# Quarter products for the last five pairs of the first layer, and a new order of work where attention ends

## The chip, the cores and the metric

One core of one Trainium2 chip runs the whole program. The metric is device time in microseconds (us) of one execution. Engines are named as in the profile: PE (TensorE matmul), PEld (its weight loads), DVE (VectorE), ACT (ScalarE), POOL (GpSimd), SP (SyncE, which issues the transfers).

## The reference

Attention (4 batches, 8 heads, 576 tokens, head size 64) whose scores are cut by a threshold near the row's maximum; then two feed-forward layers on 2304 tokens of width 512, all in fp32:

```python
scores = np.where(scores >= thresh, scores, -1e9)        # thresh = row max - tau
attn = exp(scores - max); attn = attn / (sum + 1e-09); x = attn @ v
x = (sigmoid(x @ w_gate) * (x @ w_val)) @ w_out          # d_ff 1536
h = x @ w_in                                             # d_ff 2048
y = where(h >= 1, h, where(h <= -1, 0, (h + 1)**2 / 4)) @ w2_out
```

The weights come in 64-bit floats as pairs of 32-bit words and are converted to fp32 on the chip.

## The kernel before

**Arithmetic.** Each fp32 operand of the layers is split in two parts of the matmul's input type (a high part, copied by ACT, and a low part, subtracted by DVE), and each product is three matmuls: high by high, high by low, low by high. Tokens go in three passes of 768 (T), each in two halves of 384 (HT).

**Attention** (`attention`, L200) is a generator over steps t. Pair p of heads takes five steps; N = 80 steps hold scores, and nine more drain the pipeline. `normalise` (L367) multiplies a pair's result by the reciprocal sums on POOL, 14 steps after the pair began, 12 for the last two pairs. `spread` (L361) loads the reciprocal sums, broadcast, from scratch memory: for the last pair at t = N + 3. `background` (L371) converts the first six blocks of weights in the gaps. At t = N the extraction of blocks 6 and 7 is issued and their conversion begun (`third`, four DVE operations at each of the following steps, L475).

**Layer 1** is `hidden` (L552), once for each of 36 steps s: three passes by twelve column tiles f of 128. For each half n it makes gate and value (`up`, L506: 12 matmuls of 384 columns each), the sigmoid of the gate on ACT (L567; L563 for the first tile, whose products `first_up`, L821, begins before attention has ended), the product of both on DVE (L571), its split (L572, L574). Between them it issues the split of the next tile's weights (`split_list`, L172: ACT L190, DVE L192) and some operations of `work`. Behind `hidden`, `down` (L781) multiplies the tile before by its block of w_out: 24 matmuls, four column tiles by 768 tokens, three times. Gate and value have one PSUM bank each: the next half may write one only when L567 or L571 has read it.

**Conversions** (`conversions`, L515) are the `work` of the steps: for each tile an extraction on ACT (L145), DVE operations L155 to L169, a store to scratch (`saved`). Eight operations go with each step of the first pass and six with the others (L879), so the generator ends before step 33. For layer 2 `w_sums` (L539) also makes four sums of quarter blocks of each pair of tiles and stores them in `tsaved`.

**Layer 2** is `pair` (L708), once for each of 24 pairs q: the product of 768 tokens by 512, with 512 by 256 weights, cut in 2 by 2 blocks, is made of seven block products (Winograd's form) in place of eight: 42 matmuls of 384 columns (`product`, L630), joined by copies on ACT (L730, L739) and sums on DVE (L715). `x_sums` and `w_sums` are the sums of blocks it needs. `value_steps` (L641) is the activation, `down_pair` (L764) 36 matmuls of 512 columns.

**Order of the side work in layer 2.** `due` (L665) queues steps for DVE and ACT with a time wanted, a first and a last slot and a cost; `fill` (L669) issues at four slots of a pair those that are eligible, in the order of their times, while they fit in the slot's room, and those whose last slot it is in any case. With `begin`, only steps with ACT work are taken, and the DVE step behind each gets time -1, ahead of all others. A slot is a place in the program, and each engine goes through its work in that order. At q = 0 the last tile's `down` and `finish` (L794, which copies layer 1's result out of PSUM) follow the first pair's products.

Of the kernel before, what the change touches and what calls it, by code (L numbers as in the profile page):

```python
# [10 lines left out]
F32 = mybir.dt.float32  # L11
# [18 lines left out]
def kernel(  # L30
# [63 lines left out]
    raws, wsp, pools, wsp_n, highs = {}, {}, {}, [], {}  # L94
# [105 lines left out]
    def attention():  # L200
# [166 lines left out]
        def normalise(p, s):  # L367
            x, c = x_of(p), slice(s * HS, s * HS + HS)
            nc.gpsimd.tensor_tensor(x[:, c], x[:, c], rbs[:, p % 2 * S :][:, c], op=ALU.mult)
# [33 lines left out]
        for p in range(NP):  # L403
            for i, (r, a, b) in (rounds if p + 1 < NP else final).items():
                parts.setdefault(p * U + i, []).append((p, r, range(a, b)))
        for t in range(N + 9):
# [56 lines left out]
            if t == N + 3:  # L463
                spread(NP - 1)
# [9 lines left out]
            if t > N:  # L474
                run(itertools.islice(third, 4))  # L475
            if t == N + 2:
                assert next(third, None) is None
                st2.close()
                ps_o.close()
            yield t - N, False  # L480

    def ffn(att):


        with ExitStack() as st:
# [7 lines left out]
            HC = HK * P  # L493

            def split_xs(ph, t, a, b, ks=range(KD)):

                x = xflat[:, : 2 * KD * T].rearrange("p (k i t) -> i p k t", k=KD, i=2)
                xh, xl = xsp[ph, t] = x[0], x[1]
                for c in ks:
                    src = xall[:, c, t * T + a : t * T + b]  # L500
                    nc.scalar.activation(xh[:, c, a:b], src, AF.Copy)
                    yield
                    nc.vector.tensor_tensor(xl[:, c, a:b], src, f32(xh[:, c, a:b]), op=ALU.subtract)
                    yield

            def up(ph, t, f, n, i, ps, ks=range(KD)):  # L506
                ih, il = wsp[ph, t, f][:2]
                xh, xl = xsp[ph, t]
                c = slice(n * HT, n * HT + HT)
                for kk in ks:  # L510
                    nc.tensor.matmul(ps, ih[:, i, kk], xh[:, kk, c], start=(kk == 0), stop=False)  # L511
                    nc.tensor.matmul(ps, ih[:, i, kk], xl[:, kk, c], start=False, stop=False)  # L512
                    nc.tensor.matmul(ps, il[:, i, kk], xh[:, kk, c], start=False, stop=(kk == KD - 1))  # L513

            def conversions():  # L515


                for j, (ph, f, gs) in enumerate(todo):
# [6 lines left out]
                    for m, _ in enumerate(ops):  # L525
                        if m == 3 + len(gs):
                            for g in todo[j + 2][2] if j + 2 < len(todo) else ():
                                load_w(todo[j + 2][0], g)
# [10 lines left out]
            def w_sums(j):  # L539

                b11, b21, b12, b22 = (w[:, i * HC : (i + 1) * HC] for w in w2s for i in range(2))
                t23, t14 = (x[:, 2 * KD * P :] for x in highs.values())
                t2, t3, t1, t4 = (x[:, i * HC : (i + 1) * HC] for x in (t23, t14) for i in range(2))
                for n, (o, a, b) in enumerate(((t1, b12, b11), (t2, b22, t1), (t3, b22, b12), (t4, b21, t2))):
                    nc.vector.tensor_tensor(o, a, b, op=ALU.subtract)
                    if n == 1:
                        yield
                for i, x in enumerate((t23, t14)):
                    nc.sync.dma_start(out=tsaved[j][:, i * 2 * HC : (i + 1) * 2 * HC], in_=x)
                yield  # L550

            def hidden(t, f, nxt, work):  # L552
# [5 lines left out]
                for n in range(2):  # L558
                    c = slice(n * HT, n * HT + HT)
                    act = hp_.tile([P, HT], F32, tag="act", name="act")  # L560
                    if (s := (0, t, f, n)) in early:
# [9 lines left out]
                    nc.vector.tensor_tensor(act, pv, act, op=ALU.mult)  # L571
# [14 lines left out]

            BX = 2 * HK * HT
            PRODUCTS = ((0, 0, 0, 1), (1, 1, 1, 1), (0, 2, 3, 0), (1, 3, 4, 1), (0, 4, 5, 1), (1, 5, 6, 0), (0, 6, 2, 0))

            def x_block(i):  # L590
                t = xmore[:, i * BX : (i + 1) * BX] if i < 3 else xflat[:, (i - 3) * BX :][:, :BX]
                return (t[:, : BX // 2], t[:, BX // 2 :])

            def x_sums(t):

                a11, a12, a21, a22 = (
# [4 lines left out]
                xops[t] = (a11, a12, s2, a21, s1, a22, s4)  # L601
# [4 lines left out]
            def x_split(t, i):  # L606
                a = xops[t][i]
# [3 lines left out]
            def w_split(q, i):  # L611
                w0, w1 = w32[q]
                src, a = ((w0[:, : 2 * HC], 0), (w1[:, HC : 2 * HC], 2 * HC), (tsum, 3 * HC))[i]
# [3 lines left out]
            def wout(q, i):  # L617
                s = (2 * q + i) % 4
                return wouts[s][:, 0], wouts[s][:, 1]
# [42 lines left out]
            LEN = lambda q: 11 if q == 0 else 15  # L662
            start = lambda q: sum(LEN(i) for i in range(q))

# [29 lines left out]
            def due_x(t, early=0):  # L694
                q = t * NQ
                for i in range(early, 7):
                    first = 4 * (q - 1) + (1, 1, 2, 3, 3, 3, 3)[i]
                    last = 4 * q - 1 if i < 2 else 4 * q + 1
                    due(first, last, split_steps(start(q) + i - 1, 0.84, 0.7, *x_split(t, i)))

            def due_w(q):
                at = start(q)
                for i, (when, first, last, cost) in enumerate(
                    ((-1, 4 * q - 3, 4 * q - 1, 0.6), (1.3, 4 * q - 1, 4 * q + 1, 0.32), (1, 4 * q - 1, 4 * q - 1, 1.1))
                ):
                    due(first, last, split_steps(at + when, cost, cost - 0.1, *w_split(q, i)))

            def pair(q):  # L708

                t, j = divmod(q, NQ)  # L710
                ps = [ps_a.tile([P, 512], F32, tag=f"a{i}", name="pu")[:, :HT] for i in range(2)]
                c = [(sqs[:, 1], vals[:, 0])[q % 2], (vals[:, 1], rbs, early_raw[1])[q % 3][:, :T]]
# [4 lines left out]
                more, last = q + 1 < NPASS * NQ, j == NQ - 1  # L717
                if more:
                    due_w(q + 1)
                if j == NQ - 4 and t + 1 < NPASS:  # L720
                    for i, w in enumerate(x_sums(t + 1)):
                        due(4 * q, 4 * (q + 3) - 1, [(start(q + 1) + 8 + 8 * i, 0.84, 0, True, w)])
                if last and more:
                    due_x(t + 1)
                at = start(q + 1) + 7
                for i in range(2):
                    src = w32[q][i][:, KD * P : 2 * KD * P]
                    due(4 * q, 4 * q + 5, split_steps(at - 1.8 + 0.3 * i, 0.6, 0.5, *wout(q, i), src))
# [4 lines left out]
                fill(4 * q + 1, 1.5, 1.3, small=True)  # L733
                if more:
                    load_sums(q + 1)
                if q + 2 < NPASS * NQ:
# [3 lines left out]
                fill(4 * q + 2, 0, 2.2, small=True, begin=True)  # L740
                product(3, ps)
                add(u3, ps[1], u2)
                product(4, ps)
                add(c[1][:, t1], ps[0], u3)
                product(5, ps)
                add(c[0][:, t1], ps[1], u2)
# [233 lines left out]
```

## Time and profile before

| | us |
|---|---|
| runs shown: median (lowest to highest of 3) | 1105.19 (1103.47 to 1106.47) |
| the profiled execution | 1104.5 |
| its span, first to last instruction | 1102.7 |
| attention, to the first matmul of layer 1 | about 256 |
| layer 1, to the first product of layer 2 | about 455 |
| layer 2 | about 391 |

The views are the page (shares of the whole span), the busy time by stretch, the chain of work that ended last, the timelines of single engines, and groups of instructions by line and shape. In a timeline a bracket is the idle time just before an instruction and what ended it. Times count from the span's start.

### The profile page before, as it was taken

To read this page: it belongs to the slowest core of one execution; us is meant where nothing else is said; L and a number is where in the kernel's file an instruction comes from. 1 tells how busy PE (TensorE), PEld (TensorE's weight loads), DVE (VectorE), ACT (ScalarE), POOL (GpSimd) and SP (SyncE) were. 2 spreads that over 40 slices of the span, in tenths; PEclk is the share of its full clock that TensorE was granted. 3 is DMA by queue.
4 is the path that set the end of the run, shared out by engine and by line. 5 is a ranking of instruction groups with operands and counts; after the bars stand their busy time and mean duration, and the time that the engine had idled before them with its cause. 6 is when DMAs were issued, how large, how long until landed. Compare 5 with 4: busy or idle time off the path is not lost.

```text
span 1102.7 us, 18536 instructions
## 1 busy us (share of the span) xinstructions
PE 1082.9 (98%) x6996; PEld 933.3 (85%) x6996; DVE 844.2 (77%) x1489; ACT 614.8 (56%) x1000; POOL 152.7 (14%) x315
## 2 busy tenths in 40 slices
PE   8999999999999999999999999999999999999998
PEld 6666666667899999999999999988898898888887
DVE  7999999997999988767686744576767767776663
ACT  6888888886343444333353322565566655665653
POOL 4556666552000000000000000000000000000000
PEclk9999999999999999999999999999999999999999
DMA  5344344413855566545654342223232423233301
GB/s 157 70 100 79 93 99 100 102 34 103 277 199 179 176 214 218 175 150 175 202 172 151 116 153 77 77 77 125 86 114 75 165 105 115 96 134 115 115 20 58
DMA packets 65146, 139.17 MB, mean 126 GB/s; under 512 B 9616, under 2 KB 35872, under 8 KB 65056
## 3 DMA queue, kind: packets, MB, share of 16 engines
q1 hardware_dynamic: 64912, 137.98, 39.2%
q8 instruction: 55, 0.90, 0.3%
q14 instruction: 35, 0.29, 0.1%
q10 hardware_dynamic: 144, 0.00, 0.0%
HBM read 111.15 MB, written 26.81 MB: 125 GB/s over the span
## 4 chain that ended last, share of the span: by engine, by line
PE 85%; ACT 7%; DVE 5%; issue 3%; POOL 0%; DVEq 0%; POOLq 0%; ACTq 0%
PE y L771 14%; PE pu L636 14%; PE y L789 13%; PE pgv L511 9%; PE pgv L512 9%; PE pgv L513 9%; PE av L338 6%; PE w L253 5%; PE w L306 4%; ACT ex L274 2%; PE w L249 1%; ACT sqs L645 1%; ACT sqs L646 1%; ACT hh L654 1%; DVE s L262 1%
## 5 line engine op out<-in xcount | busy, mean ns | idle before, releaser
L511 PE MATMUL pgv<-xflat,win 128*128 128x384 f32 x560 | 187.9, 336 | 3.0 <-DVE act L571 1.8
L512 PE MATMUL pgv<-xflat,win 128*128 128x384 f32 x560 | 187.9, 335 | 0.0
L513 PE MATMUL pgv<-xflat,win 128*128 128x384 f32 x560 | 187.8, 335 | 0.0
L771 PE MATMUL y<-wout,hh 128*128 128x512 f32 x576 | 184.1, 394 | 0.0
L789 PE MATMUL y<-hh,wout 128*128 128x512 f32 (+1 forms) x576 | 146.5, 336 | 0.0
L771 PEld LDWEIGHTS y<-wout,hh 128*128 128x128 f32 x576 | 108.2, 188 | 24.5
L262 DVE TENSOR_SCALAR_CACHE_REDUCE s<-w,nscale 128x576 f32<-128x576 f32 x144 | 112.2, 812 | 9.7 <-PE w L253 7.6
L571 DVE TENSOR_TENSOR act<-pgv,act 128x384 f32<-128x384 f32 x70 | 38.8, 554 | 105.2 <-PE pgv L513 104.9
L572 ACT ACTIVATE hh<-act 128x384 fp32r<-128x384 f32 x72 | 38.0, 528 | 141.7 <-DVE act L571 141.7
L771 PE MATMUL y<-wout,hl 128*128 128x512 f32 x288 | 113.6, 395 | 0.0
L282 DVE SCALAR_TENSOR_TENSOR p<-s,mx,ex 128x576 f32<-128x576 f32 x144 | 111.6, 807 | 0.0
L511 PEld LDWEIGHTS pgv<-xflat,win 128*128 128x128 f32 x560 | 105.6, 188 | 5.0 <-DVE act L571 2.1
L274 ACT ACTIVATE ex<-s,mx 128x576 f32<-128x576 f32 x144 | 104.3, 766 | 6.3 <-DVE s L262 5.9
L789 PEld LDWEIGHTS y<-hh,wout 128*128 128x128 f32 x576 | 98.1, 188 | 11.3
L512 PEld LDWEIGHTS pgv<-xflat,win 128*128 128x128 f32 x560 | 105.5, 188 | 1.6
L636 PE MATMUL pu<-xflat,win 128*128 128x384 f32 x576 | 105.2, 337 | 1.4 <-DVE sqs L715 1.1
L567 ACT ACTIVATE act<-pgv 128x384 f32<-128x384 f32 x70 | 34.2, 489 | 128.7 <-PE pgv L513 128.6
L513 PEld LDWEIGHTS pgv<-xflat,win 128*128 128x128 f32 x560 | 105.7, 189 | 0.0
L636 PEld LDWEIGHTS pu<-xflat,win 128*128 128x128 f32 x576 | 100.6, 188 | 3.1 <-DVE sqs L715 2.0
L789 PE MATMUL y<-hl,wout 128*128 128x512 f32 (+1 forms) x288 | 97.1, 337 | 0.0
L265 POOL TENSOR_SCALAR mx<-mx,tau_b 128x1 f32<-128x1 f32 x144 | 87.4, 607 | 54.7 <-DVE s L262 54.5
L253 PE MATMUL w<-qk 64*128 64x288 f32 x512 | 88.2, 430 | 2.9 <-DVE s L262 2.9
(153 smaller groups left out, 1866.0 us busy)
## 6 DMA issues: line engine op xcount, KB each, us to landing
words<-in_moe_w_out_dram SPq DMA_DIRECT2D x26, 512.0 KB
wmore<-saved SPq DMA_DIRECT2D x24, 512.0 KB
tsum<-tsaved SPq DMA_DIRECT2D x24, 512.0 KB
w<-saved SPq DMA_DIRECT2D x24, 512.0 KB
w<-saved SPq DMA_DIRECT2D x14, 768.0 KB
words<-in_moe_w_in_dram SPq DMA_DIRECT2D x16, 512.0 KB
saved<-w SPq DMA_DIRECT2D x16, 512.0 KB
wmore<-saved SPq DMA_DIRECT2D x10, 768.0 KB
```

The costliest lines, as they stand in the source:

```text
L253: nc.tensor.matmul(w[:, s, :HS], t[es, 0, u * P : u * P + P], t[es, 1, c], start=True, stop=True)
L262: nc.vector.tensor_scalar(t[:, e], w[:, :, :HS], nscale, None, op0=ALU.mult, op1=ALU.min, accum_out=mx[:, 0, e : e + 1])
L265: nc.gpsimd.tensor_scalar(mx[:, 1, e : e + 1], mx[:, 0, e : e + 1], tau_b, None, op0=ALU.add)
L274: nc.scalar.activation(ex[:, e], t[:, e], AF.Exp, scale=-1.0, bias=mx[:, 0, e : e + 1])
L282: nc.vector.scalar_tensor_tensor(pr[:, e], t[:, e].rearrange("p a b -> p (a b)"), mx[:, 1, e : e + 1], ex[:, e].rearrange("p a b -> p (a b ...
L338: nc.tensor.matmul(av[e * D : e * D + D, :n], vs[p % 3][:, e, c], rt[r][:, e, c] if c < nf else rl[r], start=c == 0, stop=c == nf,)
L511: nc.tensor.matmul(ps, ih[:, i, kk], xh[:, kk, c], start=(kk == 0), stop=False)
L512: nc.tensor.matmul(ps, ih[:, i, kk], xl[:, kk, c], start=False, stop=False)
L513: nc.tensor.matmul(ps, il[:, i, kk], xh[:, kk, c], start=False, stop=(kk == KD - 1))
L636: nc.tensor.matmul(ps[bank], l[:, k], r[:, k], start=bool(new) and k == m == 0, stop=k == HK - 1 and m == 2, skip_group_check=True,)
L771: nc.tensor.matmul(y[b], l[:, ts_], r, start=first and m == 0, stop=last and m == 2)
L789: nc.tensor.matmul(at(y, a, b), l[:, ds_], r[:, c], start=new and m == 0, stop=last and m == 2, skip_group_check=True,)
```

## The change

The last five pairs of column tiles of layer 1 (third pass, f = 2 to 11) no longer go through `hidden`. `stage` takes the place of `pair`: ten stages g come ahead of the 24 pairs of layer 2, an even one for the gates of a pair of tiles and an odd one for its values, each with seven block products of 42 matmuls. One `down` of layer 1 follows each stage from the second on, and two follow stage 10, the first pair of layer 2. The sums of weight blocks are made from the fp32 weights beside the stage before (`w_sums(g + 1)`), for layer 1 and for the first pass of layer 2, which stores them for the later passes. Gates go through the sigmoid, values through `gated_steps`. Four of the seven blocks of x are already in the tile `xflat` by its new layout or are made in its place.

Conversions now end before step 24: six operations at the first step, nine at the second, eight at each later one. Where attention ends, the whole of `third` is issued at t = N + 1, the split of tile 1's weights at step 1 in one go, then the sigmoid and product of the first half of tile 0. The last two pairs are normalised on DVE, one half with each of the steps 12 to 15; the last `spread` and the two stores of tiles 0 and 1 go behind step 1, and the loads of blocks 12 and 13 come early.

The diff, cut to its core:

```diff
-                for j in (12, 14):
-                    pn, un = divmod(t - j - i, U)
-                    if un == 0 and 0 <= pn < NP and (pn < NP - 2) == (j == 14):
-                        normalise(pn, i)
+                pn, un = divmod(t - 14 - i, U)
+                if un == 0 and 0 <= pn < NP - 2:
+                    normalise(pn, i)
...
-            if t == N + 3:
-                spread(NP - 1)
...
-            if t > N:
-                run(itertools.islice(third, 4))
+            if t == N + 1:
+                run(third)
...
                     nc.sync.dma_start(out=saved[ph, f], in_=dst)
+                    if j == 0:
+                        yield
                     if j + 1 < len(todo):
                         extract(*todo[j + 1][::2], highs[(j + 1) % 2])
                     yield
-                    if ph == 1 and f % 2 == 1:
-                        for _ in w_sums(f // 2):
-                            yield
...
+            def w_sums(g):
+                b11, b21, b12, b22 = quarters(g)
+                t2, t3, t1, t4 = (tsum[:, i * HC : (i + 1) * HC] for i in range(4))
+                q = g - N1
+                def step(n, o, a, b):
+                    nc.vector.tensor_tensor(o, a, b, op=ALU.subtract)
+                    if n == 3 and q >= 0:
+                        nc.sync.dma_start(out=tsaved[q], in_=tsum)
...
-            LEN = lambda q: 11 if q == 0 else 15
-            start = lambda q: sum(LEN(i) for i in range(q))
+            lens = [7] + [11] * (N1 - 1) + [15] * (NPASS * NQ + 1)
+            start = lambda g: sum(lens[:g])
...
+            def due_w(g):
+                at = start(g)
+                sums = g < N1 + NQ
+                if sums and g:
+                    due(4 * g - 3, 4 * g - 1, [(at - 3 + 0.1 * i, 0.4, 0, True, w) for i, w in enumerate(w_sums(g))])
                 for i, (when, first, last, cost) in enumerate(
+                    ((-3.2 if sums else -1, 4 * g - 3, 4 * g - 1, 0.6), (1.3, 4 * g - 1, 4 * g + 1, 0.32), (1, 4 * g - 1, 4 * g - 1, 1.1))
...
-                fill(4 * q + 1, 1.5, 1.3, small=True)
+                fill(4 * g + 1, 2.6 if q == 0 else 1.5, 1.3, small=True)
...
                 product(3, ps)
                 add(u3, ps[1], u2)
+                fill(4 * g + 2, 0.45, 0, small=True)
...
+                        for i in range(2):
+                            h = hts[0, NPASS - 1, F0 + 2 * n + i] = h_tiles()
+                            when = ((1.2, 1.3, 1.5), (1.25, 1.4, 1.7))[i]
+                            if q == -1:
+                                when = ((3.9, 4.2, 4.3), (6.5, 6.6, 7))[i]
+                            due(4 * g + 3, 4 * g + 7, gated_steps(c[i], cs[n][i], h, [at + x for x in when]))
+                    room = lens[g] - (4.6 if q == -1 else 5.6)
...
+            def gated_steps(c, s, h, at):
+                return [
+                    (at[0], 0.92, 0, True, lambda: nc.vector.tensor_tensor(c, c, s, op=ALU.mult)),
+                    (at[1], 0, 0.82, True, lambda: nc.scalar.activation(h[0], c, AF.Copy)),
+                    (at[2], 0.92, 0, True, lambda: nc.vector.tensor_tensor(h[1], c, f32(h[0]), op=ALU.subtract)),
+                ]
...
-                    run(itertools.islice(second, 2))
+                    run(itertools.islice(second, 6))
                     run(itertools.islice(more, {0: 4, 1: 2, 2: 2}.get(step, 0)))
+                if step == 1:
+                    pg, pv = early.pop((0, 0, 0, 0))
+                    act = acts[0, 0, 0, 0] = hp_.tile([P, HT], F32, tag="act", name="act")
+                    nc.scalar.activation(act, pg, AF.Sigmoid)
+                    nc.vector.tensor_tensor(act, pv, act, op=ALU.mult)
...
-                work = itertools.islice(conv, ops)
+                work = itertools.islice(conv, (6, 9)[s] if s < 2 else 8)
...
+                if s == 1:
+                    later.pop(0)()
+                    for f in range(2):
+                        nc.sync.dma_start(out=saved[0, f], in_=w32[0, 0, f])
...
-            for q in range(NPASS * NQ):
-                pair(q)
+            for g in range(N1 + NPASS * NQ):
+                q = g - N1
...
+                stage(g)
+                if q <= 0 < g:
+                    for x in order[NB - 2 + g : NB - 1 + g] if q else order[-2:]:
+                        down(*x[1:], y)
+                    if q == 0:
+                        finish(NPASS - 1, y)
```

Here N1 = 10 is the number of new stages, NB = 26 the number of steps left to `hidden`, F0 = 2 the first tile of the new stages, and q = g - N1.

## Rows read from the trace of the kernel before

**Rows 1.** The page's part 1, busy time of the engines over the whole span.

```profile
PE 1082.9 (98%) x6996; PEld 933.3 (85%) x6996; DVE 844.2 (77%) x1489; ACT 614.8 (56%) x1000; POOL 152.7 (14%) x315
```

**Rows 2.** By stretch: us, busy PE, PEld, DVE, ACT, POOL, clock, DMA.

```profile
278.00:280.00 2.00, 2.00 (x8) 2.00 (x9) 2.00 (x3) 1.22 (x3) 1.86 (x2) 0.53 1.00 231
...
294.25:306.76 12.51, 12.51 (x73) 11.97 (x73) 11.94 (x15) 5.20 (x9) 0.00 (x0) 1.00 0.60 195
...
431.90:582.06 150.16, 150.16 (x865) 143.71 (x865) 107.38 (x167) 56.92 (x102) 0.00 (x0) 1.00 0.52 178
...
720.00:745.00 25.00, 22.79 (x115) 19.79 (x114) 18.92 (x28) 17.14 (x29) 0.00 (x0) 1.00 0.24 85
```

**Rows 3.** The chain that ended last, layer 1 from 306 us: start, us, what.

```profile
306.76 4.19 PE y L789 x24
...
319.27 4.19 PE y L789 x24
```

**Rows 4.** The same chain in layer 2, from 804 us.

```profile
804.93 7.34 PE pu L636 x42
```

**Rows 5.** Timeline of PE where attention ends: start, us, tiles, [idle before].

```profile
268.12 0.33 PE L511 MATMUL pgv<-xflat,win 128*128 128x384 f32 x1
...
273.63 0.44 PE L511 MATMUL pgv<-xflat,win 128*128 128x384 f32 x1 [1.19 <-ACT act L567]
...
277.82 0.44 PE L511 MATMUL pgv<-xflat,win 128*128 128x384 f32 x1 [1.81 <-DVE act L571]
...
281.57 0.40 PE L789 MATMUL y<-hh,wout 128*128 128x512 f32 x1
```

**Rows 6.** Timeline of ACT in the same stretch.

```profile
269.26 0.47 ACT L563 ACTIVATE act<-w 128x384 f32<-128x384 f32 x1
...
270.88 2.33 ACT L145 ACTIVATE high<-words 128x512 f32<-128x512 f32 x4
...
273.11 0.47 ACT L567 ACTIVATE act<-pgv 128x384 f32<-128x384 f32 x1
```

**Rows 7.** Timeline of DVE in the same stretch.

```profile
275.35 0.95 DVE L155 TENSOR_SCALAR high<-high 128x1536 f32<-128x1536 f32 x1
...
276.34 0.96 DVE L157 TENSOR_SCALAR wmore<-high 128x1536 uint32<-128x1536 uint32 x1
...
277.21 0.55 DVE L571 TENSOR_TENSOR act<-pgv,act 128x384 f32<-128x384 f32 x1
```

**Rows 8.** Groups by line and shape: xcount | busy us, mean ns.

```profile
L655 DVE TENSOR_TENSOR hl<-sqs,hh 128x768 fp32r<-128x768 f32 x12 | 11.4, 951 | 0.0
...
L654 ACT ACTIVATE hh<-sqs 128x768 fp32r<-128x768 f32 x12 | 10.2, 848 | 1.8 <-DVE sqs L652 0.9
...
L190 ACT ACTIVATE win<-w 128x1024 fp32r<-128x1024 f32 x20 | 21.0, 1052 | 0.0
```

**Rows 9.** Timeline of DVE in a later step of layer 1.

```profile
298.62 1.76 DVE L169 TENSOR_TENSOR wmore<-wmore,high 128x1536 f32<-128x1536 f32 x1
...
303.18 1.22 DVE L192 TENSOR_TENSOR win<-wmore,win 128x1024 fp32r<-128x1024 f32 x1
```

**Rows 10.** Timeline of PE behind layer 2's first pair and later.

```profile
718.59 0.39 PE L789 MATMUL y<-hh,wout 128*128 128x512 f32 x1
...
726.56 1.34 PE L636 MATMUL pu<-xmore,win 128*128 128x384 f32 x6 [1.53 <-ACT act L730]
...
742.93 1.34 PE L636 MATMUL pu<-xmore,win 128*128 128x384 f32 x6 [0.34 <-ACT act L730]
...
744.61 4.46 PE L636 MATMUL pu<-xflat,win 128*128 128x384 f32 x24 [0.34 <-DVE sqs L715]
```

**Rows 11.** Timeline of DVE behind the products of that pair.

```profile
718.79 0.56 DVE L715 TENSOR_TENSOR vals<-pu,act 128x384 f32<-128x384 f32 x1 [0.49 <-PE pu L636]
...
719.86 1.28 DVE L691 TENSOR_TENSOR wout<-wmore,wout 128x512 fp32r<-128x512 f32 x2
...
721.07 0.95 DVE L652 SCALAR_TENSOR_TENSOR sqs<-sqs 128x768 f32<-128x768 f32 x1
```

More of the change, by code (lines that the diff above doesn't have):

```diff
@@ L405, in attention @@
                 parts.setdefault(p * U + i, []).append((p, r, range(a, b)))
+        later.extend((p, i, normalise) for p in (NP - 2, NP - 1) for i in range(2))
+        later.insert(0, lambda: spread(NP - 1))
         for t in range(N + 9):
@@ L559, in hidden @@
                     c = slice(n * HT, n * HT + HT)
-                    act = hp_.tile([P, HT], F32, tag="act", name="act")
-                    if (s := (0, t, f, n)) in early:
+                    done = (s := (0, t, f, n)) in acts
+                    act = acts.pop(s) if done else hp_.tile([P, HT], F32, tag="act", name="act")
+                    if done:
+                        pass
+                    elif s in early:
                         pg, pv = early.pop(s)
@@ L761, in pair @@
-                room = LEN(q) - 6.6 - (2 if j == 0 else 0)
-                fill(4 * q + 3, *((3.4, 5) if q == 0 else (room, room)))
+                at = start(g + 1)
+                if q < 0:
+                    if g % 2 == 0:
+                        sig = lambda x: nc.scalar.activation(x, x, AF.Sigmoid)
+                        due(4 * g + 3, 4 * g + 7, [(at + 1.6 + i, 0, 0.9, True, lambda x=x: sig(x)) for i, x in enumerate(c)])
+                    else:
+                        for i in range(2):
[5 more added lines that the diff above has]
+                    room = lens[g] - (4.6 if q == -1 else 5.6)
+                else:
+                    h = hts[q] = [h_tiles(), h_tiles()]
+                    at += 7
+                    for i in range(2):
+                        r = vals[:, 1] if i and not more else sqs[:, 0]
+                        if not more:
+                            when = ((-6, -4, -3.8, -3.6), (-5, -3, -2.8, -2.6))[i]
+                        elif last:
+                            when = ((-2.5, -2.4, -2.2, -2), (1, 1.2, 1.4, 1.6))[i]
+                        else:
+                            when = ((-6.2, -6.15, -5.9, -5.5), (-5.4, -5.3, -5.2, -5.1))[i]
+                        due(4 * g + 3, 4 * g + 7, value_steps(c[i], r, h[i], [at + x for x in when]))
+                    room = lens[g] - 6.6 - (2 if j == 0 else 0)
@@ L815, in store @@
                     nc.sync.dma_start(out=dst[:, a], in_=o[:, a])
-            order = [(0, t, f) for t in range(NPASS) for f in range(NF[0])]
             todo = [(0, f, range(max(3 * f, 8), 3 * f + 3)) for f in range(2, NF[0])]
@@ L846, in ffn @@
                     pools["n"] = 0
-                    for _, _, gs in todo[:2]:
-                        for g in gs:
-                            load_w(0, g)
+                    for g in range(8, 14):
+                        load_w(0, g)
                     continue
@@ L866, in ffn @@
             wmore = kp.tile([P, 6 * KD * P], F32, name="wmore")
-            n = 2 * KD * P
-            slots = [wmore[:, i * n : (i + 1) * n] for i in range(3)] + [x[:, :n] for x in ring]
+            consts = list(ring)
             n = 3 * KD * P
@@ L913, in ffn @@
                         finish(t, y)
-            for q in range(NPASS * NQ):
-                pair(q)
-                if q == 0:
-                    down(*order[-1][1:], y)
-                    finish(NPASS - 1, y)
-                elif q < NPASS * NQ - 1:
+            for g in range(N1 + NPASS * NQ):
+                q = g - N1
+                if g % 2 == 0 and g + 2 < N1:
+                    for x in order[NB + g + 2 : NB + g + 4]:
+                        load_step(*x)
+                if q == -2:
+                    n = 2 * KD * P
+                    slots = [x[:, :n] for x in ring if any(x is c for c in consts)]
+                    slots[2:2] = [wmore[:, i * n : (i + 1) * n] for i in range(3)]
+                stage(g)
[4 more added lines that the diff above has]
+                        finish(NPASS - 1, y)
+                elif 0 < q < NPASS * NQ - 1:
                     down_pair(q - 1, y)
```

203 lines of the change are left out of this document (110 added, 93 removed).

## Prediction

> **What bounds the kernel now.** I read the page first: PE is busy 98% of the span, DVE 77%, ACT 56% [rows 1]. A share of the whole span hides stages, so the busy time by stretch comes next [rows 2]. In a step of the first pass of layer 1 PE is busy in all of its 12.51 us, at the full clock (1.00, 2.4 GHz), and DVE in 11.94 of them: PE is the bound, DVE close behind. In the second pass DVE is busy 107.4 of 150.2 us. Two stretches are different. At 278 us the granted clock is 0.53, the lower of its two levels (1.2 GHz) for most of the stretch, and from 720 to 745 us PE is idle 2.2 us of 25. Elsewhere between 282 and 722 us PE never pauses, so matmuls taken out of layer 1 shorten it one for one, as long as the others keep up. The chain of waits gives the price of a step: 319.27 - 306.76 = 12.51 us, 4.19 of them the 24 matmuls of `down`, which leaves 8.32 for 48 matmuls of 384 columns [rows 3].
>
> **Seven products.** A pair of layer 2 does its 42 matmuls in 7.34 us [rows 4]. A new stage with its `down` then takes 7.34 + 4.19 = 11.53 in place of 12.51, 0.98 less; ten stages give **-9.8 us**. The number of `down`s stays the same.
>
> **Where attention ends.** PE starts tile 1 at 268.12 and then waits twice: 1.19 us for the sigmoid, 1.81 for the product L571; behind that its twelve matmuls take 281.57 - 277.82 = 3.75 us where twelve in a steady step take 8.32 / 4 = 2.08 [rows 3, 5]. The sigmoid of 273.11 stood behind four extractions (2.33 us), three of which belong to the next tile [rows 6]; the change issues these later, so the sigmoid is done by 271 and this wait goes. The product at 277.21 stood behind L155 and L157 of that next tile, 277.21 - 275.35 = 1.86 us [rows 7], which go later too. And the chain in front begins earlier: the second half of tile 0 had its sigmoid at 269.26, though its matmuls were through at about 268.3, because ACT and DVE were still at the first half; that half is now done while attention drains, and the chain moves up by 1.0. L571 then comes at 277.21 - 1.86 - 1.0 = 274.35 and the matmuls that waited start at 274.9, 0.5 us late instead of 3.0 in all. With so short a wait I expect the clock to stay up, so they take 2.08. Gain: (277.82 - 274.9) + (3.75 - 2.08) = **-4.6 us**. Bounds: 0 if another wait takes the place, -5.1 if the last 0.5 goes too.
>
> **What is late next.** With six and nine operations at the first two steps, each tile's conversion ends with its step; before, it ended two operations ahead. The split of the tile on ACT (1.05 us [rows 8]) can only follow L169, and DVE's part follows that. Before, L155, L157 and L571 stood between L169 (298.62 + 1.76 = 300.38) and DVE's split (303.18) [rows 9]; now only L571 (0.55 [rows 7]) does, so DVE idles 0.5 or a little more in each step. 11.94 + 0.5 is 12.44 of 12.51, too close to be free, and the first of these steps starts with a whole tile's operations ahead of it. I take 0.1 us in each of eight steps and 0.2 at the first: **+1.0 us**, between 0 (if L571 is late anyway) and +1.5.
>
> **The handover to layer 2.** This is the part that I expect to go wrong. Stage 9 must also make layer 2's blocks of x. Its last slot has room 6.4: three blocks (0.84 each), the two weight splits (1.1, 0.32) and two blocks more leave 0.78, less than the 0.92 of the first gated product. So in stage 10 that product, and two forced blocks of x, fill slot 41, and the ACT copy behind it (0.85 [rows 8]) is ahead of the copy that frees the bank for the fifth product. Counted from the end of the second product: 0.2 to the sum, 0.56 for it, 0.95 for the gated product, 0.85, and 0.47 for the copy itself (as the 384-wide ones [rows 6]), 3.0, against 2.1 of cover by two products: +0.9. The room of slot 41 is then used up, and the first half's subtraction, for which `down` waits at its second matmul, is issued behind the last sum and three splits, which carry time -1. In the first pair now, the same four stand ahead of L652: it begins at 721.07, 2.48 us after the `down` at 718.59 [rows 10, 11]. With 0.95 for the subtraction that is 3.4, less 0.2 for the matmul ahead: +3.2. A wait longer than those before 278 us should bring the clock down again; at the price there, +1.7. In return the wait of 1.53 at 726.56, for ACT's late copies of layer 1's result [rows 10], should go: two `down`s now cover 8.4 us of ACT's work instead of 4.2. Together 0.9 + 3.2 + 1.7 - 1.5 = **+4.3 us**, between -1.5 (all covered) and +5.8 (the old wait stays too).
>
> The Trainium skill (TensorE: Matmul & The Clock Gate, section HAM oscillation) warns that matmuls broken up by waits run at the lower clock afterwards and pay anew after each wait. By that rule the 1.7 stays in the sum. The trace agrees at 278 us and not at 726.56, where a wait of 1.53 left the clock at 1.00 [rows 2, 10]; without the 1.7 the time would be 1093.7.
>
> **What hides the stages' work.** In an odd stage DVE has five sums at 0.56 [rows 11], four weight sums (256 wide; their price is bounded by the 384-wide operation at 0.55 [rows 7]), splits of 512, 256 and 1024 elements (1.22 for 1024 [rows 9], about 2.1 together), and the four 768-wide operations of `gated_steps` at 0.95 [rows 8]: 2.8 + 2.2 + 2.1 + 3.8 = 10.9 of 11.5 us. An even one has two splits of w_out (0.64 each [rows 11]) in place of the gated four, 8.4; what an odd stage can't hold goes over to it. In layer 2's first pass the weight sums (2.2 more on DVE) lie in pairs of 15.7 us (7.34 [rows 4] and 36 matmuls of 512 columns). I cost all of it at nothing; were DVE late, the third rival gives the price.
>
> **At nothing.** Four halves normalised on DVE (288 wide, under 0.55 each) lie in steps of the second pass, where DVE has over 3 us a step free [rows 2]; without that cover they cost under 2.2. The eight operations per step there instead of six are one or two more, covered likewise. On SP, two more loads stand ahead of the store of the last pair's sums, and two stores and `spread` go behind tile 3's store; nothing but steps 12 to 15 waits for them, over 100 us later, and no wait of PE is put down to a transfer. Eight loads of `tsaved` go.
>
> **Sum.** 1104.5 (profiled execution; its span is 1102.7) - 9.8 - 4.6 + 1.0 + 4.3 = **1095.4 us**. The median of the runs is 0.7 above that execution; I leave this in the range.
>
> **Rivals.** *No wait at the handover*: if DVE comes through stage 10 before PE needs it, 1104.5 - 9.8 - 4.6 + 1.0 - 1.5 = 1089.6. For it: two `down`s in stage 10 give DVE and ACT 4.2 us more than the first pair has now. Against it: the order of issue, and the row at 721.07 [rows 11]. *Attention's end gains nothing*: another wait takes the place and the clock falls as before: 1095.4 + 4.6 = 1100.0. DVE's load of 11.94 in 12.51 speaks for it; the 3 us of idle PE against. *Each stage waits a little*: layer 2 has waits of 0.34 for L730 and again 0.34 for DVE in one pair [rows 10]; such a pair of waits in each of ten denser stages is 6.8: 1102.2, no change to speak of. *Slower*: the 1024-wide split must fit between the sixth product of a stage and the third of the next, 1.04 + 4.19 + 2.08 = 7.3 us; ACT and DVE need 1.05 + 1.22. If in the five odd stages the gated work and the weight sums went ahead of it (3.8 + 0.85 + 2.2 more), it would be 9.1, a wait of 1.8, and with a fall of the clock (1.7) 3.5 us, five times: 1095.4 + 17.5 = 1112.9. It decides from 2.5 us a stage on, where 9.1 us of gain and 3.3 more are gone. Against it: the split's place in the last slot is ahead of the gated work.
>
> **Chances.** Forecast 0.60, no handover wait 0.17, nothing at attention's end 0.10, waits in each stage 0.09, slower 0.04. About 0.3% (3.3 us) is what a measurement of this kernel can tell from no change, so below 1101.9 is faster: 0.60 + 0.17 + 0.10 = 0.87, same 0.09, slower 0.04. The range, 1088.8 to 1100.0, reaches from the second case to the third and leaves out the last two cases and the tails.
>
> **What the next profile shows.** If I am right: no clock below 1.00 around 278 us and the first `down` at about 277.0; 60 matmuls fewer; the new stages 11.5 us apart; a wait of PE of some 3 us at `down` behind stage 10's products, for a subtraction in `gated_steps`, and about 0.9 ahead of its fifth product; no long wait for L730's like in the next pair. Wrong: stages longer than 11.7, PE waiting for L571 in the first pass in total over 1.5, or stage 10 without a wait over 1.

## The result: 1095.6 us, and the profile after

The changed kernel takes 1095.59 us in the median of five runs (1095.31 to 1096.57) against 1105.65 before (1103.47 to 1106.47): a ratio of 0.9912, 95% interval 0.9898 to 0.9925. 1095.4 was forecast. The profiled execution took 1095.59 us, with a span of 1093.8 against 1102.7; the sum is checked on these two.

The page's part 1 of the changed kernel answers to [rows 1]:

```profile
PE 1072.8 (98%) x6936; PEld 922.5 (84%) x6936; DVE 898.7 (82%) x1591; ACT 632.6 (58%) x1024; POOL 149.1 (14%) x311
```

Sixty matmuls are gone, and PE's busy time with them (10.1 us); DVE has 54.5 us more to do. The new ways of waiting are in the table of PE's waits (us in total, times, longest), here without those inside attention:

```profile
PE y L863 <- DVE hl L835: 3.1, 1, 3.1
...
PE pu L667 <- ACT act L780: 1.6, 3, 0.7
...
PE pgv L516 <- DVE act L567: 0.8, 1, 0.8
PE pu L667 <- DVE vals L755: 0.7, 2, 0.4
PE pu L667 <- ACT act L789: 0.7, 1, 0.7
...
PE pu L667 <- DVE sqs L755: 0.7, 1, 0.7
PE pgv L517 <- DVE xflat L509: 0.4, 1, 0.4
```

Where they lie is in PE's timeline (start, us, tiles, [idle before]). In the order below: the end of attention, which answers to [rows 5]; a split of x for the next pass; the first product of the second new stage; stage 10 with its fifth product and `down`; the second pair of layer 2, and a wait in the third, which answer to [rows 10].

```profile
275.95 0.44 PE L516 MATMUL pgv<-xflat,win 128*128 128x384 f32 x1 [0.75 <-DVE act L567]
...
278.14 0.39 PE L863 MATMUL y<-hh,wout 128*128 128x512 f32 x1
...
562.94 0.44 PE L517 MATMUL pgv<-xflat,win 128*128 128x384 f32 x1 [0.39 <-DVE xflat L509]
...
591.93 1.32 PE L667 MATMUL pu<-xflat,win 128*128 128x384 f32 x6 [0.65 <-DVE sqs L755]
...
700.77 1.33 PE L667 MATMUL pu<-xmore,win 128*128 128x384 f32 x6 [0.73 <-ACT act L789]
...
704.02 0.39 PE L863 MATMUL y<-hh,wout 128*128 128x512 f32 x1
707.50 0.50 PE L863 MATMUL y<-hl,wout 128*128 128x512 f32 x1 [3.10 <-DVE hl L835]
...
715.79 2.25 PE L667 MATMUL pu<-xflat,win 128*128 128x384 f32 x12
...
734.39 1.32 PE L667 MATMUL pu<-xmore,win 128*128 128x384 f32 x6 [0.68 <-ACT act L780]
```

The chain that ended last shows the stages themselves (start, us, what; 42 matmuls are a stage's products, 24 its `down`), which answers to [rows 3, 4]:

```profile
649.77 7.32 PE pu L667 x42
657.09 4.19 PE y L863 x24
661.27 7.32 PE pu L667 x42
668.60 4.19 PE y L863 x24
672.79 7.35 PE pu L667 x42
...
700.24 0.48 ACT act L789
...
704.22 0.56 DVE vals L755
704.77 0.60 DVE win L722
705.37 1.21 DVE wout L722 x2
706.58 0.88 DVE hl L835
```

A stage is 11.51 us (672.79 - 661.27 = 11.52) where a step was 12.51. The last four lines are why `down` waits: DVE's last sum, then three weight splits, and only then the subtraction that makes `hl`. The last view is the clock by stretch (us, busy PE, PEld, DVE, ACT, POOL, clock, DMA), which answers to [rows 2]:

```profile
278.00:280.00 2.00, 2.00 (x13) 1.78 (x12) 1.41 (x3) 1.03 (x3) 0.00 (x0) 1.00 0.81 336
294.00:306.51 12.51, 12.51 (x74) 11.97 (x73) 11.75 (x15) 5.11 (x10) 0.00 (x0) 1.00 0.86 293
706.00:708.00 2.00, 0.50 (x2) 0.46 (x3) 2.00 (x3) 0.00 (x0) 0.00 (x0) 1.00 0.00 0
708.00:710.00 2.00, 2.00 (x13) 1.73 (x13) 1.09 (x2) 1.65 (x2) 0.00 (x0) 1.00 0.00 0
```

It no longer falls at 278 us, and in this execution not behind the wait of 3.10 us either.

Cut at PE's own marks (attention's last run of sixteen transposes, at 252.51 us before and 253.20 after, called its last transposes here, though a few short ones follow; the first `down`; 24 steps later; the first product of layer 2's second pair; the last matmul), the two executions compare like this:

| stretch | before, us | after, us | change | forecast |
|---|---|---|---|---|
| start to attention's last transposes | 252.51 | 253.20 | +0.69 | 0 |
| to the first `down` | 29.06 | 24.94 | -4.12 | -4.6 |
| 24 steps | 300.32 | 301.47 | +1.15 | +1.0 |
| ten steps or stages and the handover | 140.89 | 136.18 | -4.71 | -4.0 |
| the rest of layer 2 | 375.81 | 373.88 | -1.93 | -1.5 |

The sum is -8.9 against -9.1. The total is nearly exact and no line of it is, so the experiments look at the lines.

### The profile page after: what moved, and what is told of

Same layout as the page of the kernel before. It is cut to its first block, busy times and chain, and to the rows that moved or that the text cites. A ratio compares the mean times of both kernels' runs of the same rounds, so it can differ in the third digit from the quotient of the medians.

```text
span 1093.8 us, 18529 instructions
## 1 busy us (share of the span) xinstructions
PE 1072.8 (98%) x6936; PEld 922.5 (84%) x6936; DVE 898.7 (82%) x1591; ACT 632.6 (58%) x1024; POOL 149.1 (14%) x311
## 4 chain that ended last, share of the span: by engine, by line
PE 84%; ACT 7%; DVE 6%; issue 2%; POOL 0%; DVEq 0%; POOLq 0%; ACTq 0%
PE pu L667 21%; PE y L845 15%; PE y L863 13%; PE pgv L517 6%; PE pgv L516 6%; PE av L338 6%; PE pgv L518 6%; PE w L253 5%; PE w L306 4%; ACT ex L274 2%; PE w L249 2%; DVE xflat L722 1%; ACT hh L685 1%; ACT xall L348 1%; DVE win L722 1%
## 5 line engine op out<-in xcount | busy, mean ns | idle before, releaser
L667 PE MATMUL pu<-xflat,win 128*128 128x384 f32 x816 | 159.8, 337 | 1.4 <-DVE vals L755 0.7
L667 PEld LDWEIGHTS pu<-xflat,win 128*128 128x128 f32 x816 | 143.5, 188 | 5.8 <-DVE vals L755 1.4
L516 PE MATMUL pgv<-xflat,win 128*128 128x384 f32 x400 | 133.9, 335 | 0.8 <-DVE act L567 0.8
L517 PE MATMUL pgv<-xflat,win 128*128 128x384 f32 x400 | 133.9, 335 | 0.4 <-DVE xflat L509 0.4
L518 PE MATMUL pgv<-xflat,win 128*128 128x384 f32 x400 | 133.7, 334 | 0.0
L667 PE MATMUL pu<-xmore,win 128*128 128x384 f32 x612 | 123.7, 336 | 2.4 <-ACT act L780 1.6
L667 PEld LDWEIGHTS pu<-xmore,win 128*128 128x128 f32 x612 | 107.8, 188 | 4.3 <-ACT act L780 3.3
L314 ACT ACTIVATE r<-w 128x1024 f32<-128x1024 f32 x64 | 65.2, 1018 | 29.8 <-PE w L306 29.4
L568 ACT ACTIVATE hh<-act 128x384 fp32r<-128x384 f32 x52 | 27.3, 524 | 94.8 <-DVE act L567 94.8
L253 PEld LDWEIGHTS w<-qk 64*128 64x128 f32 x512 | 49.2, 187 | 34.5 <-DVE s L262 20.0
L338 PE MATMUL av<-r,v 128*64 128x320 f32 (+1 forms) x512 | 75.8, 418 | 1.8 <-ACT xall L348 1.1
```

Of the source, the lines that this page charges most:

```text
L253: nc.tensor.matmul(w[:, s, :HS], t[es, 0, u * P : u * P + P], t[es, 1, c], start=True, stop=True)
L338: nc.tensor.matmul(av[e * D : e * D + D, :n], vs[p % 3][:, e, c], rt[r][:, e, c] if c < nf else rl[r], start=c == 0, stop=c == nf,)
L516: nc.tensor.matmul(ps, ih[:, i, kk], xh, start=(kk == 0), stop=False)
L517: nc.tensor.matmul(ps, ih[:, i, kk], xl, start=False, stop=False)
L518: nc.tensor.matmul(ps, il[:, i, kk], xh, start=False, stop=(kk == KD - 1))
L667: nc.tensor.matmul(ps[bank], l[:, k], r[:, k], start=bool(new) and k == m == 0, stop=k == HK - 1 and m == 2, skip_group_check=True,)
```

## Experiments

Each was timed in five rounds beside the kernel before (medians of 1105.15 to 1105.78 us there).

**One half of the change each.** `att_only` has the new order where attention ends and leaves the last ten steps of layer 1 as they were; `stages_only` has the ten stages and leaves the end of attention as it was. The diffs are cut to their core.

```diff
 att_only, from the changed kernel:
-            N1 = 10
...
 stages_only, from the changed kernel:
-                    run(itertools.islice(second, 6))
+                    run(itertools.islice(second, 2))
...
-                work = itertools.islice(conv, (6, 9)[s] if s < 2 else 8)
+                work = itertools.islice(conv, 8)
```

> The kernel before with the new order where attention ends, without the new stages. Theory (the two parts are independent, and this one is worth what the two traces show between the end of attention and the first `down`, 4.1 us): 1105.6 - 4.1 = 1101.5 us, the granted clock 1.00 around 278 us, one wait of PE for the product L571 of some 0.7 us. Rival (what is gained there is lost again in the first pass, where DVE is busy 96%): within 1 us of the kernel before. Up to 0.4 us may come back where the first pass splits x for the second.

> The changed kernel with the old order where attention ends. Theory: ten stages save 9.8, the waits of 0.65, 0.73 and 3.10 us behind stages 0 and 10 stay, and the wait of 1.53 us in layer 2 stays away: the traces give -4.5 for the stages and the handover and -2.1 behind it, so 1105.6 - 6.6 = 1099.0 us, with up to 0.7 more for the splits of x. At 278 us the clock falls again and PE waits 3.0 us. Rival (the stages' gain needs the earlier end of attention, through conversions that end sooner): 1102 us or more.

`att_only` took 1101.40 us (ratio 0.9965, 0.9952 to 0.9979), as expected. `stages_only` took 1101.42 (0.9957, 0.9944 to 0.9970), 2.4 more than expected, but one of its five runs took 1098.04. That run has a mean clock of 0.998, as most runs of the kernel before have with their one fall at attention's end; the other four have 0.995. The profiled one shows why, in the busy times and clock of two stretches of `stages_only` around the wait of 3.10 us for `hl`, which is there too:

```profile
708.00:710.00 2.00, 0.19 (x1) 0.00 (x0) 2.00 (x4) 0.00 (x0) 0.00 (x0) 1.00 0.00 0
...
712.00:714.00 2.00, 2.00 (x9) 1.83 (x8) 1.09 (x3) 1.84 (x3) 0.00 (x0) 0.50 0.00 0
```

PE is idle at 708 us and its clock is at the lower level (0.50) at 712. From the first matmul of `down` to the next product it takes 14.40 us (707.80 to 722.20) where the changed kernel took 11.77 (704.02 to 715.79). So a fall at the handover is real, and its price here was 2.6 us. It also explains why the halves don't add up: they gain 3.8 us each, 7.6 together, where the whole change gained 10.1.

**The wait for `hl`.** `hl_last` puts, in the first of the two `down`s at the handover, all matmuls on `hh` ahead of those on `hl`; `longer_wait` puts four more operations on DVE ahead of `hl`, whose results nobody reads.

```diff
 hl_last:
-                for a, b, d in spans:
+                for k, (a, b, d) in [(k, x) for k in ((0, 2), (1,)) for x in spans] if late else [((0, 1, 2), x) for x in spans]:
...
 longer_wait:
+                if q == 0:
+                    for _ in range(4):
+                        add(u3, u2, u2)
```

> In stage 10 the first `down` takes the products with the low part of h last, after sixteen others (2.8 us); nothing else is changed. Theory (PE waits 3.10 us there only because the second matmul needs the late subtraction): the wait falls to about 0.5 us, 1095.6 - 2.5 = 1093.1 us. Rival (DVE and ACT are behind as a whole, and the next pair waits for what this one no longer waits for): the time stays within 0.7 us of 1095.6, with a wait of 2 us or more in the next pair.

> Four more sums of 384 columns on DVE ahead of the splits behind stage 10's products, so that the wait of 3.10 us becomes 5.0. Theory of the prediction (a wait longer than those before 278 us brings the clock down, only not far enough above them here): the clock falls behind it in all runs, for 1.1 to 1.7 us more than the 1.9 of the sums, 1098.6 to 1099.2 us. Rival (the length of the wait does not decide alone, and the fall at 278 us had other conditions): the clock stays at 1.00 in some of the runs, and those take 1097.5 us.

`hl_last` took 1093.68 us (0.9894, 0.9881 to 0.9908), 1.9 below the changed kernel, with the clock at 0.999 or 1.00 in all of its runs. Its PE timeline:

```profile
703.86 2.96 PE L865 MATMUL y<-hh,wout 128*128 128x512 f32 x16
707.35 1.67 PE L865 MATMUL y<-hl,wout 128*128 128x512 f32 x8 [0.52 <-DVE hl L835]
709.10 0.51 PE L865 MATMUL y<-hh,wout 128*128 128x512 f32 x1
710.09 0.50 PE L865 MATMUL y<-hl,wout 128*128 128x512 f32 x1 [0.49 <-DVE hl L835]
```

Sixteen matmuls now cover most of the wait: 0.52 is left, and 0.49 in the second `down` for its own `hl`, which the long wait had hidden. `longer_wait` took 1099.40 us (0.9945, 0.9933 to 0.9958); its wait is 5.34 us, 2.24 more for four operations at 0.56, and the mean clock was 0.998 or less in all five runs. Of the 3.8 us that it lost, 2.2 are the operations; the rest is about what a fall costs (from `down` to the next pair the trace has 15.31 us, 2.24 + 1.30 more than the changed kernel). The wait is on the path, one for one.

**The copy ahead of the fifth product.** `hh_after_u2` moves the last pair's `hh` copy on ACT behind the copy that frees the bank.

```diff
-                fill(4 * g + 1, 2.6 if q == 0 else 1.5, 1.3, small=True)
+                fill(4 * g + 1, 2.6 if q == 0 else 1.5, 0.8 if q == 0 else 1.3, small=True)
```

> The changed kernel (1095.6 us) with the last pair's `hh` copy placed behind the stage's second sum on ScalarE's list instead of ahead of it (one slot's room cut from 1.3 to 0.8 in the first product stage of layer 2 alone). Theory: the copy of 0.85 us delays the sum's read of the bank that the fifth product needs, so that wait of 0.73 us goes, and `hl` moves ahead of the three weight splits on VectorE, so that `down` waits for it 1.4 us instead of 3.1: 1093.2. Rival: VectorE's order stays, `hl` comes at its old time and the 0.73 us saved only lengthen the wait behind: 1095.6; or the copy comes later by as much as it stood ahead and `hl` with it: 1096.3.

1092.93 us (0.9885, 0.9872 to 0.9899), close to the theory's 1093.2, though its sum held only in part. DVE's timeline shows the new order:

```profile
703.56 0.56 DVE L755 TENSOR_TENSOR vals<-pu,act 128x384 f32<-128x384 f32 x1 [0.15 <-PE pu L667]
704.03 0.95 DVE L835 TENSOR_TENSOR hl<-rb,hh 128x768 fp32r<-128x768 f32 x1
704.90 1.28 DVE L722 TENSOR_TENSOR wout<-w,wout 128x512 fp32r<-128x512 f32 x2
```

`hl` stands directly behind the last sum, and PE waits 1.29 us for it, 1.81 less. One part was wrong: the fifth product no longer waits, but the sixth now does, 0.66 us in place of 0.73, for a sum on DVE that is late next. PE's timeline of these two products:

```profile
699.31 1.20 PE L667 MATMUL pu<-xmore,win 128*128 128x384 f32 x6
701.17 1.31 PE L667 MATMUL pu<-xflat,win 128*128 128x384 f32 x6 [0.66 <-DVE high L755]
```

From the end of the 24 steps to layer 2's second pair the profiled executions are 2.04 us apart (136.18 and 134.14). The other 0.8 of their difference lies at the start and in the rest of layer 2, where this edit changes nothing; that the total met the theory is in part luck.

**The first two steps.** `phase87` gives them eight and seven conversion operations instead of six and nine; `no_early` leaves the product of the first tile's first half where it was.

```diff
 phase87:
-                work = itertools.islice(conv, (6, 9)[s] if s < 2 else 8)
+                work = itertools.islice(conv, (8, 7)[s] if s < 2 else 8)
 no_early:
-                if step == 1:
-                    pg, pv = early.pop((0, 0, 0, 0))
...
```

> The changed kernel (1095.6 us) with eight and seven conversion operations in the first two steps instead of six and nine, all else as it is. Theory: the gain where attention ends (4.1 us to the first `down`) is in part the two operations of step 0 that no longer stand ahead of the gate's product on VectorE, 1.2 to 1.9 us; with them back TensorE waits for that product 1.5 to 2.5 us in step 1 rather than 0.75, and the clock may fall as it did before: 1096.9, or 1098.5 with a fall. Rival: the early gate and its product alone make the gain, and two operations are hidden by the 2.3 us that VectorE has spare there: 1095.6.

> The changed kernel (1095.6 us; 1095.4 in runs at full clock) without the early sigmoid and product of the first tile's first half in step 1, which go back to their place behind the second half's matmuls. Theory: the 4.1 us gained at attention's end come from two sources, the two conversion operations that moved from step 0 to step 1 (about 0.9 us, by the kernel with eight and seven) and this early product; without it TensorE waits for the product some 1.7 us instead of 0.75, the first `down` starts 1.0 us later: 1096.6, up to 1098 in runs where the clock falls. Rival: the two conversion operations and the fewer steps of unused work ahead of them make all of the gain, and the early product only stands where it would have waited: 1095.6.

`phase87`: 1097.20 us (0.9925, 0.9913 to 0.9938); its runs at full clock took 1096.41 and 1096.60, about 1.0 more than those of the changed kernel. From attention's last transposes to the first `down` it needs 278.76 - 252.93 = 25.83 us, 0.89 more. Its two waits in PE's timeline:

```profile
273.51 0.44 PE L516 MATMUL pgv<-xflat,win 128*128 128x384 f32 x1 [0.64 <-ACT act L562]
276.57 0.45 PE L516 MATMUL pgv<-xflat,win 128*128 128x384 f32 x1 [0.69 <-DVE act L567]
```

The sigmoid's wait of before is back, and it and the product's wait are both short. `no_early`: 1096.90 us (0.9919, 0.9904 to 0.9934), but its one run at full clock took 1095.87, and from the last transposes to the first `down` it needs 278.49 - 253.51 = 24.98 us, the same as the changed kernel's 24.94. The rival holds: the early product brings nothing. ACT in the trace of `no_early`:

```profile
267.05 0.44 ACT L348 ACTIVATE xall<-av 128x320 f32<-128x320 f32 x1 [2.07 <-PE av L338]
267.38 0.49 ACT L558 ACTIVATE act<-w 128x384 f32<-128x384 f32 x1
...
269.66 0.49 ACT L558 ACTIVATE act<-w 128x384 f32<-128x384 f32 x1 [0.64 <-PE w L518]
```

The first sigmoid follows the last attention copy at once. Before, two weight splits of 0.62 us stood between them on ACT (at 266.38 and 266.90); the change issues six operations of the split of tile 1's weights, not two, with each step in which attention drains, so they are out of the way. That this, and not the early product, moved the chain up is read from the traces; it was not tried alone.

**The longer steps.** `conv_even` moves conversion operations out of the two steps in which x is split for the next pass.

```diff
-                work = itertools.islice(conv, (6, 9)[s] if s < 2 else 8)
+                work = itertools.islice(conv, {0: 6, 1: 9, 11: 4, 23: 2}.get(s, 9 if 13 <= s < 23 else 8))
```

> The changed kernel (1095.6 us) with the conversion operations of the second pass spread another way: nine in the steps 13 to 22, four and two in the two steps that also split the next pass's activation, eight elsewhere as now. Theory: the 1.15 us that the first-pass steps lost at 403 to 429 and at 541 to 567 us is TensorE reading pieces of the activation that VectorE splits late, behind eight conversion operations of the same step; with four and two there the steps are 12.51 again: 1094.4. Rival: the pieces are late because of their source (the accumulator that ScalarE's copy reads), not because of the conversions: 1095.6, with the same longer steps; or nine in a step is too much and steps 13 to 22 become longer: above 1095.6.

All steps are 12.51 us again: from the first `down` to the one 24 steps later 578.24 - 277.92 = 300.32 us, 1.15 less than in the changed kernel. The median, 1095.69 us (0.9908, 0.9893 to 0.9923), hides it: three of the four runs have a mean clock of 0.997 or 0.998, and the fourth, at 1.00, took 1093.69. The profiled run, one of the three, shows a fall at the handover, in its clock at 706 us:

```profile
706.00:708.00 2.00, 1.98 (x7) 1.78 (x8) 1.09 (x2) 1.13 (x2) 0.00 (x0) 0.50 0.00 0
```

**Cover for the second stage.** `cover01` puts four spans of the last step's `down` between the first two stages.

```diff
+                if g == 0:
+                    down(*order[NB - 1][1:], y, spans[:4])
...
-                        down(*x[1:], y)
+                        down(*x[1:], y, spans[4:] if g == 1 else spans)
```

> The changed kernel (1095.6 us) with half of a `down` (four of its spans, the other half where it was) put between the first two product stages. Theory: the 0.65 us wait of the second stage's first product for the last sum of the first (at 592 us) is there because nothing else stands between the two on TensorE, so 2.1 us of `down` cover it: 1094.9, and no wait at 592. Rival: the sums of the first stage are late as a whole, the stages behind it only inherit the delay, and the 0.65 comes back one stage later: 1095.6.

1097.17 us (0.9924, 0.9910 to 0.9937). The wait at 592 us is gone and a longer one stands a stage later, in PE's timeline of `cover01`:

```profile
605.84 1.34 PE L667 MATMUL pu<-xmore,win 128*128 128x384 f32 x6 [1.36 <-ACT act L780]
```

That is the rival, and worse than it. As I read the trace, the half of `down` that is missing behind the second stage had covered ACT and DVE there; this was not tried alone. The stages take 0.6 us more, and there is a fall at the handover (13.29 us from `down` to the next pair, not 11.77); all five runs had a mean clock of 0.998.

**The three good edits together.** `best2` has the diffs of `conv_even`, `hh_after_u2` and `hl_last`.

> The changed kernel with three of the edits tried alone: the other spread of conversion operations, the `hh` copy behind the second sum, and in the last pair's `down` all `hh` matmuls ahead of those on `hl`. Theory: the waits are in series on TensorE, so the gains add: 1092.9 with the copy moved, less 1.15 for the first-pass steps and less 1.3 for the wait for `hl`, which 48 of the 72 matmuls now cover: 1090.5, with the clock at 1.00 in all runs. Rival: VectorE is late behind the handover as a whole, so what `down` no longer waits for the next product stage does: 1091.8.

1092.09 us (1091.85 to 1092.57; 0.9875, 0.9858 to 0.9891), below both kernels, with a mean clock of 1.00 in all runs. It is 1.6 above the theory's figure and nearer to the rival's 1091.8. PE's timeline of `best2` shows the gain of `hl_last` shrunk:

```profile
705.39 1.56 PE L865 MATMUL y<-hl,wout 128*128 128x512 f32 x8
707.22 0.49 PE L865 MATMUL y<-hh,wout 128*128 128x512 f32 x1 [0.27 <-ACT hh L834]
708.21 0.50 PE L865 MATMUL y<-hl,wout 128*128 128x512 f32 x1 [0.50 <-DVE hl L835]
```

The first `down`'s `hl` is in time, but the second `down` now waits for its own `hh` and `hl`, 0.77 us in all where 1.29 was to be saved. The 1.1 us of the steps came in full (300.32 again), so 1.1 + 0.5 = 1.6 should have come on top of `hh_after_u2`; by the medians it was 0.8. The two profiled executions show where the rest went: 0.2 in a later start, 0.2 in longer stages, 0.2 at the handover, and 0.6 in layer 2 behind it (374.10 against 373.51), 0.03 in nearly every pair. Why layer 2 varies like that stays open.

## Why the prediction was right, and where it was not

**The total** was right by luck, because errors of both signs met: a fall of the clock that did not come in this execution (-1.7) and 0.4 more gained in the rest of layer 2, against 0.5 less at attention's end, 0.7 at the start, 0.65 at the second stage, and what each wait costs beside its idle time. The execution from which the sum starts, 1104.5, also lay 1.15 below the median of the five runs before; by the medians the gain is 10.1, not 9.1.

**Seven products**: right. Stages are 11.51 us apart, 1.0 less than a step, ten times -10.0 against -9.8.

**Where attention ends**: size right (-4.1 against -4.6), one cause wrong. The sigmoid's wait is gone, the product comes as two operations fewer would have it, the remaining wait is 0.75 where 0.5 was forecast, and the clock stays up. But the step "that half is now done while attention drains, and the chain moves up by 1.0" named the wrong mover: without the early product the chain is as early. It moved up 0.7, by ACT's two splits that no longer stand there.

**What is late next**: the term was +1.0 and 1.15 came, but as another thing. In the steps of the first pass where the term was placed PE never waits, though DVE is busy 11.75 of 12.51 us. The loss is around the end of the first pass (0.2 in its last step and 0.2 in the next) and at the end of the second (0.7), where x is split for the next one. DVE's timeline shows the second split, before and twice after:

```profile
414.37 1.96 DVE L503 TENSOR_TENSOR xflat<-xall,xflat 128x384 fp32r<-128x384 f32 x4
...
411.22 1.96 DVE L509 TENSOR_TENSOR xflat<-xall,xflat 128x384 fp32r<-128x384 f32 x4
...
562.34 1.96 DVE L509 TENSOR_TENSOR xflat<-xall,xflat 128x384 fp32r<-128x384 f32 x4
```

At the end of the first pass DVE begins it 7.95 us behind the step's `down` (411.22 - 403.27), where it was 7.66 before (414.37 - 406.71). The 0.2 in the next step is the product L567, which ends at 426.49 us, just before PE's next product at 426.54; conversions, a half normalised on DVE and copies of layer 1's result stand ahead of it. At the end of the second pass the split begins 8.47 us behind `down` (562.34 - 553.87). There it is an item that stood under "at nothing": eight operations per step in place of six were not "covered likewise", since 3 us of room on the average say nothing of the one step that has them ahead of pieces that PE reads at once. `stages_only`, whose conversions end two operations earlier, begins this split 6.61 us behind `down` (564.90 - 558.29) and loses nothing in that step.

**The handover**: the working held. The fifth product waited 0.73 (0.9 forecast), `down` 3.10 (3.2 forecast), in the order read from the code, and the old wait of 1.53 is gone. Each wait costs more than its idle time: `down` starts its second matmul at 707.50, 3.48 us behind the first instead of 0.23, which is 3.25, and its third 0.34 behind that, so 0.11 more. (Part of this is the way of counting: the idle time starts at the end of the matmul before, 0.39 us behind its start, while without a wait the next one starts after 0.23.) Over three waits this is the 0.8 by which the stages' stretch exceeds -10.0 + 0.65 + 0.73 + 3.10 = -5.5.

**The step that failed** is "a wait longer than those before 278 us should bring the clock down again; at the price there, +1.7". By their mean clock of 0.998 it did so in two of the changed kernel's five runs, which take 1.1 us more (1096.55 and 1096.57 against 1095.31 to 1095.59). The rule that the prediction cites from the Trainium skill (TensorE: Matmul & The Clock Gate, section HAM oscillation) is told there of waits about as long as this one and longer, each of which brings the clock down. So the wait of 1.53 us at 726.56, which left the clock up, does not speak against it, and here, at 3.10 us, the fall followed in some runs and not in others. The price was of the right size, 1.4 us in `conv_even` (702.54 to 715.69 is 13.15, less 11.77) and 2.6 in `stages_only`.

**Not foreseen**: the 0.65 us at the second stage. Between the first two stages there is no `down`, so the first product must wait until the last sum has read its bank. Of the rivals, "each stage waits a little" and "slower" are refuted by stages 11.51 us apart, "no wait at the handover" by the 3.10 us, and "attention's end gains nothing" by the 4.1 us and by `att_only`.

## What to carry to other kernels

When a stage gets shorter, read the order of issue behind its last product: an operation that only fills room there can stand ahead of what the next matmul needs, and moving one copy gained another 2.0 us in the stretch that it touches, where the whole change had gained 10. Look for cover step by step, not by the average of a pass, above all where one step does something that the others don't. When a wait may bring the clock down, compare runs of the same clock, since a real gain of 1.15 us can vanish in a median.

## Not expected of the hardware

The same wait of 3.10 us at the same place left the clock up in some runs and not in others. Counted by the mean clock, which does not say where it fell, 20 of the 28 runs of the six kernels that have this wait show a fall beyond that at attention's end, where there is one (2 of 5 in the changed kernel, 5 of 5 in `cover01`); all five runs with 5.34 us do; none of the twelve runs of `hl_last`, `hh_after_u2` and `best2` does, whose longest wait there is 1.29. What decides between them at 3.10 us stays open. The fall at attention's end was no certainty either: 3 of the 25 runs of the kernel before that were taken beside the experiments have a mean clock of 1.00. The fall also lasted differently: 3 to 4 us in `conv_even`, nearly 7 in `stages_only`. And attention varies by itself: its last transposes begin at 252.82 to 253.51 us in the profiled executions of the changed kernel and of the eight kernels that differ from it only behind that point; their first group of matmuls takes 4.11 to 4.64 us.
